# A gated mix of attention and a long convolution on one core: a planned instruction order with wider margins for loads and for TensorE's instruction blocks

## The chip, the cores and the metric

One core of a Trainium2 chip. The metric is the device time of one execution in microseconds (us); lower is better. Five engines run their own queues in order: TensorE (PE, with PEld for its weight loads), VectorE (DVE), ScalarE (ACT), GpSimd (POOL) and SyncE (SP), which here issues nearly all DMAs.

## What is computed

```python
x = A_x                                              # 1 x 2048 x 512
g = sigmoid((x * gate_w).sum(-1, keepdims=True))
# A: softmax attention, 32 heads of 16
q, k, v = split(x @ wqkv)
a = (softmax(q @ k.T / 4) @ v) @ wo
# B: a causal convolution along the sequence, one kernel of 2048 taps for each of 512 channels
K = einsum("dn,dnl,dn->dl", C, exp(dt * A * l), dt * B).real     # 128 complex poles for each channel
b = irfft(rfft(x, padded) * rfft(K, padded)) + x * Dskip         # y[t] = sum over s of K[t - s] x[s]
out = g * a + (1 - g) * b
```

## The kernel before

**Attention.** There are 32 heads x 16 key blocks of 128 x 4 query blocks of 512, that is 2,048 score tiles of 128 x 512. Three tiles make a group; there are 683 groups, numbered g. For a group, PE writes the scores into one of two banks (SC<-Qm,KT, three matmuls that run side by side), ACT takes the exponential (ET or EX<-SC, L1001), and later PE multiplies by the values into the bank OA, four matmuls of 32 columns side by side, called a quad (OA<-ET,VE). In some groups the third tile does not go to ACT: DVE makes a 16-bit exponent from the scores (DZ<-SC, L1023) and POOL makes three shifted copies (DU<-DZ, L1037). PE sums all four (OA<-DZ,VE and OA<-DU,VE). Four such tiles are a set, and it costs four quads where one would have done. So a group has an exponential of three tiles (128 x 1536) or of two (128 x 1024).

**Background.** Everything else on PE writes the one bank MB, and is put between the groups: the projections of Q, K and V, the convolution's taps (MB<-T,Z, `kstage`), the convolution itself (MB<-U,H, `ystage`; U holds 16 shifted rows of x, H the taps, and each of 32 passes v uses one U and four H, numbered u = 4v to 4v + 3) and the output (`outs`: MB<-Wo,OnR and MB<-Yl,idb, 16 row blocks lt of 128). U and H are loaded from DRAM on SP's queue (L1518, L1530) into rings; from u = 48 on the ring of H has 8 buffers, before that 4. A load is issued when the last reader of its buffer is done and, if it is paced, when a certain exponential is done. Qm is the query block with the rows of every second head zero; it is loaded from DRAM (`mk_qm`, L857), with its zeros kept in SBUF. The convolution's result goes Yst -> gm_yd -> Yl.

**What sets the order.** A planner in Python runs while the kernel is built. `Prog` keeps a clock of each engine; `Sched.fill` takes, after each group's exponential, the earliest ready piece of any thread (`ystage`, `kstage`, `outs`, ...) and appends it to its engine's queue. PE, ACT, DVE and SP run in the order so written. A load counts as landed at its reckoned end plus a margin, `DMARG` = 1.6 us. The planner also counts PE's instructions in blocks of 256; `land()` is the time at which it reckons the next block to be there. A background piece that would start with few instructions left before the block's edge is held until then:

```python
k = self.p.edge() - len(self.p.pt) - 2 * sum(isinstance(a, tuple) for a in t.seg)
if t.up > 0:
    e = max(e, self.p.land() - t.cost - max(k - KEEP, 0) / FORE)
room = max(0, want - self.p.act - own) * ZCOL
if e + t.cost + room > pe_until and t.up > 0 or e > min(until, pe_until):
    continue
```

`want` is the number of columns that PE should stream in a group (`FILL` for each 1.335 us of ACT). What lacks is filled with matmuls of zeros (OA<-wm, SC<-wm); it is set for groups below `ZEND` = 200 only. `PACE` gives by which group how many sets should have been begun; `decide` begins one when DVE's clock allows.

Of the kernel before, what the change touches and what calls it, by code (L numbers as in the profile page):

```python
# [13 lines left out]
P = 128  # L14
# [22 lines left out]
OUTP = 6  # L37
YSEG = 4
KSEG = 4
FILL = 1550  # L40
FILL2 = 1550
OVER = 0.5
# [4 lines left out]
DMARG = 1.6  # L47
SPLAG = .8
# [13 lines left out]
PACE = ((0, 0), (40, 0), (90, 0), (140, 1.0), (200, 10.0), (270, 24.0), (340, 35.9), (420, 51.9), (500, 71.9), (570, 89.4), (630, 104.4), (683, 114.47))  # L62
# [3 lines left out]
XGO = 'g30'  # L66
YGO = 'projs'
YLGO = 'K15'
BG0 = 'g0'
# [4 lines left out]
KP = 1  # L74
# [6 lines left out]
US = (2, 12, 3)  # L81
HS = (4, 48, 8)
BACK = 0.4
UN4 = 4
# [11 lines left out]
KEEP = 8  # L96
FORE = 12
# [442 lines left out]
def declare(nc, es):  # L540
# [84 lines left out]
    for n, free in (("kd", 8 * NBLK * HR * HW), ("xs", T * D * UW), ("yd", 2 * D * S), ("qd", D * S), ("od", D * S)):  # L625
        B[n] = Buf(n, "dr", free, BF16)
        B[n].t = nc.dram_tensor("gm_" + n, [free // P, P], BF16)
# [100 lines left out]
def record(nc, p, B, ins):  # L728
# [122 lines left out]
    def mk_qm(b, j):  # L851
# [575 lines left out]
    def kstage(blk):  # L1427
# [8 lines left out]
        for k in range(8):  # L1436
            for t in range(4):
# [4 lines left out]
                for j in range(4):  # L1442
                    x = k ^ j
                    ch = 32 * (blk % 4) + 4 * (j // 2) + 2 * (j % 2) + 8 * (x % 4) + x // 4
# [4 lines left out]
            if k == 0:  # L1449
                yield ("PE", .06)  # L1450
                for j in range(4):
                    mm(lambda j=j: MB(0, [[64, 4], [256, 2]], 32 * j, 32), lambda: sel(0, [[1, 32]]), lambda j=j: Dr(32 * blk + 4 * (j // 2) + 2 * (j % 2), [[8, 4], [1, 2]]),
                       [(sel, 0), (sel, 1), (Dr, 0), (Dr, 1)], ky, False, False, pos=(0, 32 * j), c=.06 if j == 0 else 0, a=2, cfg="C")
# [40 lines left out]
    UN = 4 * UW - R8 + 1  # L1494
    UP = 16 * UW // UN4

# [12 lines left out]
    def yloads():  # L1509
        yield ("AFTER", YGO)  # L1510
        for v in range(2 * NBLK):
# [4 lines left out]
            for i in range(UN4):  # L1516
                yield ("SP", .7)
                dma("SP", lambda e, v=v, U=U, i=i: e.dma_start(U(UP * i, [[1, UN]]),  # L1518
                                                               xs.dram((v // 2 * 32 + v % 2 * 4) * UW + 2 * UP * i + R8 - 1, [[D * UW, T], [-1, R8], [1, UN]])),
                    [(xs, (v // 8, s0)) for s0 in range(0, T, 4)], [(U, i, v)], c=.62, lat=3.5, b=UB * 2 / UN4, pace=True)  # L1520
            for q in range(4):
# [5 lines left out]
                for i in range(HN):  # L1527
# [3 lines left out]
                        [(kd, (u // 8, u // 2 % 4))], [(H, i, u)], c=.6, lat=3.5, b=HB / HN, pace=True)  # L1531
                sch.mark(f"yl{u}")

    def ystage():
        for u in range(2 * NBLK):
# [26 lines left out]
            op("DVE", lambda v, w=w, h=h: v.tensor_tensor(Yst(1024 * w + 4 * h, [[128, R8], [8, 16], [1, 4]]), MB(0, [[1, R8], [R8, 16], [NC, 4]]),  # L1562
# [7 lines left out]
    def yout(blk):  # L1570
# [7 lines left out]
        for k, y in enumerate((Yl, Yl2)):  # L1578
            yield ("SP", .6, YLP)
            n = 128 >> k  # L1580
            dma("SP", lambda e, k=k, y=y, n=n: e.dma_start(y(4 * n * blk, [[n, 4], [1, n]]), yd.dram(512 * blk + 8192 * k, [[8192 * 2, P], [128, 4], [1, n]])),
                [(yd, (blk, j)) for j in range(4)], [(y, blk)], c=.6, lat=3, b=.5, pace=True)
# [58 lines left out]
    def out_y(lt, bank, k, wide=False):  # L1641
        b, off, sl = bank
        y, at, W = ((Yl, 8 * lt, 128), (Yl2, 8 * (lt - 8), 64))[k]
        strips(wide, lambda p, n: b(off, [[1, 512]], p, n), lambda p, n: idb(p, [[1, n]]), lambda: y(at, [[W, D // 8], [1, 8]]),
               [(idb, 0)] + [(y, x) for x in range(NBLK)], [(b, sl, ('o', lt))], False, k == 1 and lt < 12)
# [5 lines left out]
    def outs():  # L1651
# [16 lines left out]
        for lt in range(13):  # L1668
# [13 lines left out]
            if lt < 8:  # L1682
                op("DVE", lambda v, lt=lt, o=o, off=off: v.scalar_tensor_tensor(o(off, [[1, D]]), MB(0, [[1, D]]), B["g"](lt, [[1, 1]]),
                                                                                Yl(8 * lt, [[128, D // 8], [1, 8]]), ALU.mult, ALU.add),
                   [(MB, 0, ('o', lt))] + [(Yl, k) for k in range(NBLK)] + key("g"), W, c=.7)
# [238 lines left out]
```

## Time and profile before

| | us |
|---|---|
| runs, median of 3 | 759.11 (756.84 to 760.77) |
| profiled execution | 762.17 |
| its span | 760.4 |
| ACT busy | 735.7 |
| PE busy | 688.9 |
| DVE busy | 656.1 |
| POOL busy | 363.4 |
| DMA queue q1, share of 16 engines | 49.8% |

Busy time is the sum of an engine's records. The profile calls time "issue" in which an engine waited for nothing that it shows. Rows of windows give, for each engine, its busy time and in brackets the number of its instructions, and at the end the granted TensorE clock (1.00 is full speed), the DMA share and GB/s.

### The profile page before, as it was taken

To read this page: it belongs to the slowest core of one execution; us is meant where nothing else is said; L and a number is where in the kernel's file an instruction comes from. 1 tells how busy PE (TensorE), PEld (TensorE's weight loads), DVE (VectorE), ACT (ScalarE), POOL (GpSimd) and SP (SyncE) were. 2 spreads that over 40 slices of the span, in tenths; PEclk is the share of its full clock that TensorE was granted. 3 is DMA by queue.
4 is the path that set the end of the run, shared out by engine and by line. 5 is a ranking of instruction groups with operands and counts; after the bars stand their busy time and mean duration, and the time that the engine had idled before them with its cause. 6 is when DMAs were issued, how large, how long until landed. Compare 5 with 4: busy or idle time off the path is not lost.

```text
span 760.4 us, 31203 instructions
## 1 busy us (share of the span) xinstructions
PE 688.9 (91%) x13820; PEld 288.1 (38%) x13821; DVE 656.1 (86%) x1091; ACT 735.7 (97%) x694; POOL 363.4 (48%) x358
## 2 busy tenths in 40 slices
PE   8778877987898899999999998989999999999997
PEld 3222332432454443445444433524443444222222
DVE  8999997899998898889879868988887878787884
ACT  7999999999999999999999978999999999999995
POOL 5000000100053455565536545586778777777674
PEclk9999999999999999999999989999999999999999
DMA  9656561441554767646578788216356576110001
GB/s 206 157 110 123 110 99 32 112 107 40 163 131 101 203 182 191 185 110 158 132 180 231 177 216 210 65 41 175 107 126 158 126 193 148 36 32 20 25 16 36
DMA packets 177769, 94.45 MB, mean 124 GB/s; under 512 B 117857, under 2 KB 161250, under 8 KB 177634
## 3 DMA queue, kind: packets, MB, share of 16 engines
q1 hardware_dynamic: 175618, 91.28, 49.8%
q8 instruction: 108, 1.77, 1.0%
q10 hardware_dynamic: 2016, 1.18, 0.7%
q14 instruction: 27, 0.22, 0.1%
HBM read 63.29 MB, written 18.90 MB: 108 GB/s over the span
## 4 chain that ended last, share of the span: by engine, by line
ACT 82%; PE 12%; DVE 2%; POOL 2%; DMA 1%; issue 1%; POOLq 0%; SPq 0%; DVEq 0%
ACT ET L1001 74%; ACT EX L1001 7%; PE OA L743 5%; PE SC L743 5%; PE MB L743 2%; POOL DU L1037 2%; DMA H<-gm_kd 1%; DVE DZ L1023 1%; DVE T L1082 0%; DVE ON L1073 0%; ACT L1001 0%; ACT L1773 0%; POOLq L705 0%; SPq L1530 0%; DVEq L705 0%
## 5 line engine op out<-in xcount | busy, mean ns | idle before, releaser
L1001 ACT ACTIVATE ET<-SC 128x1024 bf16<-128x1024 f32 (+1 forms) x616 | 670.9, 1369 | 10.5 <-PE SC L743 8.9
L1037 POOL INT64_ADD DU<-DZ x339 | 352.3, 1054 | 384.1 <-DVE DZ L1023 195.9
L1023 DVE TENSOR_SCALAR DZ<-SC 128x512 uint16<-128x512 f32 x452 | 302.6, 685 | 72.1 <-PE SC L743 66.1
L743 PE MATMUL SC<-Qm,KT 32*128 32x512 bf16 x2048 | 274.7, 388 | 55.7 <-ACT ET L1001 50.7
L743 PEld LDWEIGHTS SC<-Qm,KT 32*128 32x128 bf16 x2048 | 70.0, 91 | 262.3 <-ACT ET L1001 202.3
L743 PE MATMUL OA<-ET,VE 128*32 128x512 bf16 x1456 | 151.0, 392 | 0.0
L743 PE MATMUL OA<-DU,VE 128*32 128x512 bf16 x1356 | 132.0, 388 | 1.6 <-POOL DU L1037 1.5
L743 PEld LDWEIGHTS MB<-U,H 128*32 128x32 bf16 x4096 | 83.9, 144 | 29.5 <-issue 19.3
L743 PE MATMUL MB<-U,H 128*32 128x88 bf16 (+7 forms) x4096 | 91.1, 226 | 3.3 <-issue 1.7
L1001 ACT ACTIVATE EX<-SC 128x1024 bf16<-128x1024 f32 (+1 forms) x67 | 71.5, 1277 | 0.0
L1082 DVE TENSOR_TENSOR T<-B,DT 128x1536 bf16<-128x1536 bf16 x64 | 64.0, 1035 | 0.2 <-issue 0.2
L743 PEld LDWEIGHTS OA<-ET,VE 128*32 128x32 bf16 x1456 | 39.0, 95 | 59.8 <-issue 56.5
L743 PE MATMUL OA<-wm 128*32 128x256 bf16 (+3 forms) x318 | 56.0, 346 | 1.2 <-DVE idf L793 1.2
L743 PEld LDWEIGHTS OA<-DU,VE 128*32 128x32 bf16 x1356 | 35.5, 97 | 44.5 <-issue 34.2
L743 PEld LDWEIGHTS MB<-T,Z 128*32 128x32 bf16 x2048 | 44.8, 154 | 11.2 <-issue 6.9
L743 PE MATMUL MB<-T,Z 128*32 128x64 bf16 (+1 forms) x2048 | 47.5, 235 | 0.1
L743 PE MATMUL OA<-DZ,VE 128*32 128x512 bf16 x452 | 45.6, 393 | 0.0
L1082 DVE TENSOR_TENSOR ft<-Z 128x512 f32<-128x512 f32 (+3 forms) x48 | 39.4, 845 | 0.3
L1082 DVE TENSOR_TENSOR Z<-ft,ft 128x1024 bf16<-128x1024 bf16 (+3 forms) x56 | 33.1, 591 | 0.7
L1058 DVE STREAM_TRANSPOSE OT<-OA 128x512 f32<-128x512 f32 x32 | 22.7, 708 | 5.9 <-PE OA L743 5.8
L1562 DVE TENSOR_TENSOR Yst<-MB,gt 128x512 bf16<-128x512 f32 x32 | 21.8, 682 | 4.3 <-PE MB L743 4.3
L1082 DVE TENSOR_TENSOR ft<-Z,DM 128x1024 bf16<-128x1024 bf16 x32 | 22.3, 714 | 0.0
(128 smaller groups left out, 401.6 us busy)
## 6 DMA issues: line engine op xcount, KB each, us to landing
H<-gm_kd SPq DMA_DIRECT2D x128, 256.0 KB, 4.2
U<-gm_xs SPq DMA_DIRECT2D x128, 134.2 KB, 3.7
T<-B SPq DMA_DIRECT2D x16, 256.0 KB, 2.9
gm_yd<-Yst SPq DMA_DIRECT2D x64, 64.0 KB, 2.8
gm_kd<-Ks SPq DMA_DIRECT2D x64, 40.0 KB, 2.8
gm_xs<-xP SPq DMA_DIRECT2D x16, 136.0 KB, 4.3
gm_pd<-L SPq DMA_DIRECT2D x8, 256.0 KB, 4.3
Z<-gm_pd SPq DMA_DIRECT2D x8, 256.0 KB, 3.6
```

What stands on the lines that cost most here:

```text
L743: op("PE", lambda t: t.matmul(out(), lhsT(), rhs(), start=start, stop=stop, skip_group_check=True, **kw), R, W, c=c, lat=.15, a=a, cfg=cfg)
L1001: op("ACT", lambda a: a.activation(E(at, [[1, 512 * n]]), sc(0, [[1, 512 * n]]), AF.Exp, scale=DH ** -0.5), [(sc, i, g) for i in range(n)] ...
L1023: op("DVE", lambda v: v.tensor_scalar(z.u16(512 * k, [[1, 512]]), sc(1024, [[1, 512]]), XS, XB, ALU.mult, ALU.add), [(sc, 2, g)], [(z, k, ...
L1037: op("POOL", lambda v, u=u, cut=cut: v.int64_add(u.u64(), z.u64(), cut * 0x0001000100010001), R, [(u, 0, i)], c=1.016, lat=.09, lk=True)
L1058: op("DVE", lambda v: v.transpose(OT(512 * w, [[1, 512]]), OA(0, [[1, 512]])), [(OA, 0, b)], [(OT, w, b)], c=.64)
L1082: op(eng, lambda v: v.tensor_tensor(o(), a(), b_(), f), R, W, c=c)
L1562: op("DVE", lambda v, w=w, h=h: v.tensor_tensor(Yst(1024 * w + 4 * h, [[128, R8], [8, 16], [1, 4]]), MB(0, [[1, R8], [R8, 16], [NC, 4]]), ...
```

## The change

The change alters the planner's numbers, some transfers and the layout of three buffers; the whole order is then planned anew.

- Numbers: `KEEP` 8 to 36 and `FORE` 12 to 15, so that a background piece is held back when fewer than 36 instructions of the block would be left, not 8. `FILL` 1550 to 1500, `OVER` 0.5 to 0.3. From group 200 on `want` is no longer 0 but follows `LOW` = 1150, with a surplus of up to `SURP` = 1200 columns carried over. `PACE` is changed; 114 sets are begun, not 113. Priorities (`OUTP`, `KP`) and starts (`XGO`, `BG0`, `YLGO`) are changed.
- The margin of U loads from v = 12 and of H loads from u = 48 on is `HM` = 5 us.
- Qm comes by one transfer of 128 rows, not four of 16; its zero rows lie in DRAM, written by four new transfers (`qzeros`). U comes in two pieces of 1081 columns, not four of 537. Yl is loaded in two halves with shorter runs, 64 transfers and not 32. The channels are put in another order for this (`ch`, Yst, Yl).

```diff
-FILL = 1550
-FILL2 = 1550
-OVER = 0.5
+FILL = 1500
+FILL2 = 1500
+OVER = 0.3
+LOW = 1150
+SURP = 1200
+HM = 5
-UN4 = 4
+UN4 = 2
-KEEP = 8
-FORE = 12
+KEEP = 36
+FORE = 15
...
     def mk_qm(b):
-            dma("SP", lambda e: e.dma_start(Qm(512 * w, [[1, 512]], 32 * j + 16 * w, 16),
-                                            B["qd"].dram(((4 * qc + pi) * P + 32 * j + 16 * w) * 512, [[512, 16], [1, 512]])),
-                [(B["qd"], (pi, qc))], [(Qm, (w, j), b)], c=.62, lat=2.8)
+            dma("SP", lambda e: e.dma_start(Qm(512 * w, [[1, 512]]),
+                                            B["qd"].dram((2 * (4 * qc + pi) * P + 16 * w) * 512, [[64 * 512, 4], [512, 32], [1, 512]])),
+                [(B["qd"], (pi, qc)), (B["qd"], ('z', qc))], [(Qm, (w, j), b) for j in range(4)], c=.55, lat=2.9, b=.45)
...
     def yloads():
-                                                               xs.dram((v // 2 * 32 + v % 2 * 4) * UW + 2 * UP * i + R8 - 1, [[D * UW, T], [-1, R8], [1, UN]])),
-                    [(xs, (v // 8, s0)) for s0 in range(0, T, 4)], [(U, i, v)], c=.62, lat=3.5, b=UB * 2 / UN4, pace=True)
+                                                               xs.dram(16 * v * UW + UP * i + R8 - 1, [[D * UW, T], [-1, R8], [1, UN]])),
+                    [(xs, (v // 8, s0)) for s0 in range(0, T, 4)], [(U, i, v)], c=.62, lat=3.5, b=UB * 2 / UN4, m=HM if v >= US[1] else DMARG, pace=True)
-                        [(kd, (u // 8, u // 2 % 4))], [(H, i, u)], c=.6, lat=3.5, b=HB / HN, pace=True)
+                        [(kd, (u // 8, u // 2 % 4))], [(H, i, u)], c=.6, lat=3.5, b=HB / HN, m=HM if u >= HS[1] else DMARG, pace=True)
...
     def yout(blk):
-            n = 128 >> k
-            dma("SP", lambda e, k=k, y=y, n=n: e.dma_start(y(4 * n * blk, [[n, 4], [1, n]]), yd.dram(512 * blk + 8192 * k, [[8192 * 2, P], [128, 4], [1, n]])),
+            n = 64 >> k
+            for h in range(2):
+                dma("SP", lambda e, k=k, y=y, n=n, h=h: e.dma_start(y(4 * n * (2 * blk + h), [[n, 4], [1, n]]), yd.dram(512 * blk + 8192 * k + 64 * h, [[8192 * 2, P], [128, 4], [1, n]])),
...
+    def qzeros():
+        for c in range(4):
+            yield ("AFTER", QZ[c])
+            yield ("SP", .6, 1)
+            dma("SP", lambda e, c=c: e.dma_start(B["qd"].dram((8 * c * P + 16) * 512, [[32 * 512, 32], [512, 16], [1, 512]]), wm(0, [[0, 16], [1, 512]], 0, 32)),
+                [(wm, 0)], [(B["qd"], ('z', c))], c=.6, lat=3.5, b=2.0, pace=c > 0)
...
     for g in range(NG):
-        want = (FILL if g < REST[3] else FILL2) * (t - t0) / 1.335 + min(max(lack, -256), 768)
+        want = (FILL if g < ZEND else LOW) * (t - t0) / 1.335 + min(max(lack, -256 if g < ZEND else -SURP), 768)
-        sch.fill(t, t + OVER, want if g < ZEND else 0)
-        lack = want - p.act if g < ZEND else 0
+        sch.fill(t, t + OVER, want)
+        lack = want - p.act
```

The order of the queues changes all over the program. Three places follow; buffer numbers stand behind the names.

The first is SP's queue where loads 76 to 79 of H are issued (H4 to H7), with U1 of their pass ahead of them. Before:

```order
L1518 DMA U1_161<-gm_xs 128x1x537 x2
L1574 DMA gm_yd<-Yst_171 32x8x128 x4
L1518 DMA U1_161<-gm_xs 128x1x537 x2
L1530 DMA H4_167<-gm_kd 128x1x1024
L1530 DMA H5_168<-gm_kd 128x1x1024
L1530 DMA H6_169<-gm_kd 128x1x1024
L1530 DMA H7_170<-gm_kd 128x1x1024
L1518 DMA U2_162<-gm_xs 128x1x537 x2
L857 DMA Qm_52<-gm_qd 16x512 x4
L1518 DMA U2_162<-gm_xs 128x1x537 x2
```

and after:

```order
L1522 DMA U1_161<-gm_xs 128x1x1081
L1751 DMA gm_qd<-wm_89 32x16x512
L1522 DMA U1_161<-gm_xs 128x1x1081
L1534 DMA H4_167<-gm_kd 128x1x1024
L861 DMA Qm_52<-gm_qd 128x1x512
L1534 DMA H5_168<-gm_kd 128x1x1024
L1534 DMA H6_169<-gm_kd 128x1x1024
L1534 DMA H7_170<-gm_kd 128x1x1024
L1578 DMA gm_yd<-Yst_171 32x8x128 x4
L1522 DMA U2_162<-gm_xs 128x1x1081 x2
```

The issues of U and Qm have become fewer rows of the same bytes or more, and a new write of zeros (gm_qd<-wm) stands among them. By the planner's group numbers H4 is issued in group 359 and first read in 364 before; it is issued in 362 and first read in 380 after.

The second is PE's queue at the convolution's loads 84 and 85 (H4 and H5, with U0). Before (groups 382 and 383):

```order
L743 MATMUL MB<-U0_160,H4_167 32x72 x4
L743 MATMUL SC0<-Qm_52,KT_49 128x512 x3
L743 MATMUL MB<-U0_160,H5_168 32x128 x4
L743 MATMUL MB<-U0_160,H5_168 32x120 x4
L743 MATMUL MB<-U0_160,H5_168 32x112 x4
L743 MATMUL MB<-U0_160,H5_168 32x104 x4
L743 MATMUL MB<-U0_160,H5_168 32x96 x4
L743 MATMUL MB<-U0_160,H5_168 32x88 x4
L743 MATMUL MB<-U0_160,H5_168 32x80 x4
L743 MATMUL MB<-U0_160,H5_168 32x72 x4
L743 MATMUL MB<-U0_160,H6_169 32x128 x4
L743 MATMUL MB<-U0_160,H6_169 32x120 x4
```

and after (groups 397 to 400):

```order
L747 MATMUL OA<-DU02_60,VE_53 32x512 x4
L747 MATMUL SC1<-Qm_52,KT_49 128x512 x3
L747 MATMUL MB<-U0_160,H4_167 32x96 x4
L747 MATMUL MB<-U0_160,H4_167 32x88 x4
L747 MATMUL MB<-U0_160,H4_167 32x80 x4
L747 MATMUL MB<-U0_160,H4_167 32x72 x4
L747 MATMUL OA<-DU03_61,VE_53 32x512 x4
L747 MATMUL SC0<-Qm_52,KT_49 128x512 x3
L747 MATMUL OA<-ET_54,VE_53 32x512 x4
L747 MATMUL OA<-DU00_58,VE_53 32x512 x4
L747 MATMUL SC1<-Qm_52,KT_49 128x512 x3
L747 MATMUL OA<-DZ01_57,VE_53 32x512 x4
```

Before, 64 convolution matmuls stand in a row behind the scores SC0, of which the first 40 and more are shown; after, runs of 16 stand with two or three score groups between them.

The third is the end of PE's queue, from the last score group on. Before:

```order
L743 MATMUL SC0<-Qm_52,KT_49 128x512 x2
L743 MATMUL OA<-DZ13_65,VE_53 32x512 x4
L743 MATMUL MB<-Wo_79,OnT3_72 32x512 x8
L743 MATMUL OA<-DU13_69,VE_53 32x512 x4
L743 MATMUL MB<-Yl_101,idb_93 32x512 x4
L743 MATMUL OA<-ET_54,VE_53 32x512
L743 MATMUL OA<-EX_55,VE_53 32x512 x3
L743 MATMUL MB<-Yl2_102,idb_93 32x512 x4
L743 MATMUL OA<-DU14_70,VE_53 32x512 x4
L743 MATMUL OA<-DU15_71,VE_53 32x512 x4
L743 MATMUL SC1<-Wo_79,OnT3_72 128x512 x3
L743 MATMUL OA<-EX_55,VE_53 32x512 x4
```

and after:

```order
L747 MATMUL OA<-DU13_69,VE_53 32x512 x4
L747 MATMUL MB<-Wo_79,OnR2_75 32x512 x4
L747 MATMUL MB<-Yl_101,idb_93 32x512 x4
L747 MATMUL MB<-Yl2_102,idb_93 32x512 x4
L747 MATMUL OA<-DU14_70,VE_53 32x512 x4
L747 MATMUL OA<-ET_54,VE_53 32x512 x4
L747 MATMUL OA<-DU15_71,VE_53 32x512 x4
L747 MATMUL MB<-Wo_79,OnT3_72 32x512 x12
L747 MATMUL MB<-Yl_101,idb_93 32x512 x4
L747 MATMUL MB<-Yl2_102,idb_93 32x512 x4
L747 MATMUL SC1<-Wo_79,OnT3_72 128x512 x3
L747 MATMUL OA<-ET_54,VE_53 32x512 x4
```

The output's matmuls into MB for row block 12 (OnT3, Yl, Yl2) stood ahead of the last two sums (DU14, DU15); they now stand behind them, since row block 11 is only finished there.

More of the change, by code (lines that the diff above doesn't have):

```diff
@@ L65 @@
 YQ = 0
-XGO = 'g30'
+XGO = 'g50'
 YGO = 'projs'
-YLGO = 'K15'
-BG0 = 'g0'
+YLGO = 'K14'
+BG0 = 'g30'
 BG1 = 'K1'
@@ L73 @@
 TP = 2
-KP = 1
+KP = 0.2
 NB = 2
@@ L80 @@
 NZ = 2
-US = (2, 12, 3)
-HS = (4, 48, 8)
+US = [2, 12, 3]
+HS = [4, 48, 8]
 BACK = 0.4
-UN4 = 4
+UN4 = 2
+QZ = ('g6', 'g80', 'g200', 'g360')
 HN = 1
@@ L1561, in ystage @@
             yield ("DVE", .7, -1)
-            op("DVE", lambda v, w=w, h=h: v.tensor_tensor(Yst(1024 * w + 4 * h, [[128, R8], [8, 16], [1, 4]]), MB(0, [[1, R8], [R8, 16], [NC, 4]]),
+            op("DVE", lambda v, w=w, h=h: v.tensor_tensor(Yst(1024 * w + 64 * h, [[128, R8], [4, 16], [1, 4]]), MB(0, [[1, R8], [R8, 16], [NC, 4]]),
                                                 B["gt"](0, [[16, R8], [1, 16], [0, 4]]), ALU.mult),
@@ L1642, in out_y @@
         b, off, sl = bank
-        y, at, W = ((Yl, 8 * lt, 128), (Yl2, 8 * (lt - 8), 64))[k]
-        strips(wide, lambda p, n: b(off, [[1, 512]], p, n), lambda p, n: idb(p, [[1, n]]), lambda: y(at, [[W, D // 8], [1, 8]]),
-               [(idb, 0)] + [(y, x) for x in range(NBLK)], [(b, sl, ('o', lt))], False, k == 1 and lt < 12)
+        y, at, W = ((Yl, 4 * lt, 64), (Yl2, 4 * (lt - 8), 32))[k]
+        strips(wide, lambda p, n: b(off, [[1, 512]], p, n), lambda p, n: idb(p, [[1, n]]), lambda: y(at, [[W, D // 4], [1, 4]]),
+               [(idb, 0)] + [(y, (x, h)) for x in range(NBLK) for h in range(2)], [(b, sl, ('o', lt))], False, k == 1 and lt < 12)
     def out_dma(lt, q="SP"):
```

35 lines of the change are left out of this document (18 added, 17 removed).

## The prediction

> **What bounds the kernel now.** I read the page first (busy shares, chain), then the exponentials by shape, then ACT's and PE's time line where ACT stands idle, then the clock window by window. "L1001" is the exponential of the scores, SC the score banks, OA the attention sums, MB the bank of all other matmuls, which I call background.
>
> ```profile
> PE 688.9 (91%) x13820; PEld 288.1 (38%) x13821; DVE 656.1 (86%) x1091; ACT 735.7 (97%) x694; POOL 363.4 (48%) x358
> ACT 82%; PE 12%; DVE 2%; POOL 2%; DMA 1%; issue 1%; POOLq 0%; SPq 0%; DVEq 0%
> ```
>
> ACT bounds: 97% busy and 82% of the chain. The groups of ACT by shape, then pieces of the chain and of ACT's time line (start, length, count):
>
> ```profile
> L1001 ACT ACTIVATE ET<-SC 128x1024 bf16<-128x1024 f32 x392 | 378.4, 1190 | 9.4 <-PE SC L743 7.9 <-PE OA L743 1.1
> L1001 ACT ACTIVATE ET<-SC 128x1536 bf16<-128x1536 f32 x224 | 310.2, 1682 | 1.1 <-PE SC L743 1.0
> L1001 ACT ACTIVATE EX<-SC 128x1024 bf16<-128x1024 f32 x61 | 63.3, 1239 | 0.0
> L1001 ACT ACTIVATE EX<-SC 128x1536 bf16<-128x1536 f32 x6 | 9.6, 1672 | 0.0
> ...
> 11.18 1.45 ACT ET L1001
> 13.15 57.76 ACT ET L1001 x43
> 569.13 6.42 ACT ET L1001 x7
> 746.42 3.54 ACT L1001 ACTIVATE EX<-SC 128x1024 bf16<-128x1024 f32 x3
> ```
>
> Records overlap, so the pace is read from unbroken runs: 57.76/43 = 1.343 us for three tiles, 6.42/7 = 0.917 us for two. 453 exponentials of two and 230 of three need 415.4 + 308.9 = 724.3 us. They run from 11.18 to 746.42 + 3.54 = 749.96, 738.8 us, of which some 0.8 is two small ACT instructions. So 13.7 us are lost between them; 11.2 before and 10.4 behind are head and tail of the 760.4 us span.
>
> Where the 13.7 us lie: ACT in two stretches of 100 us, and the shapes in the second.
>
> ```profile
> 280.00:380.00 100.00, 99.53 (x99) 1.00 0.60 153
> 380.00:480.00 100.00, 91.89 (x90) 0.93 0.79 199
> L1001 ACT ACTIVATE ET<-SC 128x1024 bf16<-128x1024 f32 x68 | 65.6, 1086 | 7.5 <-PE SC L743 6.7 <-PE OA L743 0.7
> L1001 ACT ACTIVATE ET<-SC 128x1536 bf16<-128x1536 f32 x22 | 31.4, 1525 | 0.6 <-PE SC L743 0.5
> ```
>
> 68 x 0.917 + 22 x 1.343 = 91.9: 8.1 us are lost from 380 to 480, where the granted clock is 0.93. The other 640 us lose 5.6, some 0.9 in 100. What stopped PE there, from the time lines of SP, PE and ACT (last bracket: idle before, and releaser) and the chain:
>
> ```profile
> 387.19 4.67 DMA H<-gm_kd
> 433.53 3.10 SPq L1530 DMA_DIRECT2D H<-gm_kd  x4
> 437.73 0.45 PE L743 MATMUL MB<-U,H 128*32 128x128 bf16 x16 [1.72 <-issue]
> 438.54 1.97 ACT L1001 ACTIVATE ET<-SC 128x1024 bf16<-128x1024 f32 x2 [1.47 <-PE SC L743]
> 460.11 1.14 PE L743 MATMUL MB<-U,H 128*32 128x128 bf16 x64
> 464.87 0.39 PE L743 MATMUL SC<-Qm,KT 32*128 32x512 bf16 x2 [0.69 <-issue]
> ```
>
> The reader is to see two causes. First, a convolution matmul stands in PE's queue ahead of scores and waits for its H: issued at 433.53, used at 437.73, 4.2 us later; the chain has the same wait from 387.19. Second, behind a burst of 64 background matmuls PE stands 0.69 us for "issue" in the middle of three scores, which wait for no data that the profile shows. The clock then adds to both (PE busy is the first figure, granted clock the third from the end):
>
> ```profile
> 67.95:71.36 3.41, 2.20 (x30) 0.65 (x26) 3.37 (x6) 3.41 (x4) 0.00 (x0) 1.00 0.60 85
> 71.36:74.78 3.42, 3.42 (x35) 0.85 (x32) 2.48 (x5) 3.42 (x3) 0.00 (x0) 0.50 0.17 21
> 95.26:98.67 3.41, 2.25 (x70) 1.01 (x57) 3.36 (x7) 3.41 (x4) 0.00 (x0) 1.00 0.13 12
> ...
> 388.80:392.22 3.42, 2.04 (x35) 0.67 (x34) 3.35 (x7) 3.42 (x4) 0.00 (x0) 1.00 0.79 189
> ...
> 436.59:440.00 3.41, 2.07 (x70) 1.42 (x70) 1.65 (x3) 1.94 (x3) 3.03 (x3) 1.00 1.07 252
> 463.90:467.31 3.41, 2.03 (x14) 0.48 (x12) 2.77 (x6) 2.69 (x3) 2.80 (x3) 1.00 0.42 121
> 467.31:470.72 3.41, 3.41 (x27) 0.76 (x30) 2.07 (x5) 2.21 (x3) 1.30 (x2) 0.50 0.91 235
> ```
>
> A stretch of 3.41 us with PE busy for 2.0 to 2.2 is followed by one at half clock; the row of 2.25 is the lowest that is not. From 380 to 480 a clock of 0.93 is 7 us of full clock missing, four such stretches of 1.7, after the three rows that stand there.
>
> **The change, part by part.** (1) One more set of tiles goes from ACT to DVE (114 sets for 113). The program has 457 exponentials of two tiles and 226 of three: 419.1 + 303.5 = 722.6, so -1.7 us on the path. What the set adds elsewhere, by the page:
>
> ```profile
> L1037 POOL INT64_ADD DU<-DZ x339 | 352.3, 1054 | 384.1 <-DVE DZ L1023 195.9 <-DVE T L1082 95.9 <-DVE ft L1082 41.1
> L1023 DVE TENSOR_SCALAR DZ<-SC 128x512 uint16<-128x512 f32 x452 | 302.6, 685 | 72.1 <-PE SC L743 66.1
> H<-gm_kd SPq DMA_DIRECT2D x128, 256.0 KB, 4.2
> U<-gm_xs SPq DMA_DIRECT2D x128, 134.2 KB, 3.7
> Yl<-gm_yd SPq DMA_DIRECT2D x16, 128.0 KB, 3.1
> Yl<-gm_yd SPq DMA_DIRECT2D x16, 64.0 KB, 3.3
> DMA to landing us min/median/max: 3.1/4.2/6.8
> ```
>
> DVE gets 4 x 0.685 = 2.7 us, POOL 3 x 1.054 = 3.2, PE three quads of matmuls. DVE is 86% and POOL 48% busy, so ACT covers them; without that cover they would be the 2.7 us.
>
> (2) Loads are asked for earlier (HM). The last row is H alone, issue to landing. Counted in score groups between an H load's place in SP's order and its first matmul, 14 of the 80 loads from number 48 on have 5 or 6 groups before, 4.6 to 5.5 us at 0.917; now three have 7 (6.4 us), 77 have 8 or more. So nearly all stand beyond the 6.8 us maximum. SP is relieved: 120 + 128 + 32 = 280 issues of Qm, U and Yl become 30 + 64 + 64, with four of zeros, all in the queue that issues H. A U of double size should land near H's 4.2 us (256 KB); its nearest first use is 6 groups off. The 32 more Yl loads land in 3.1 to 3.3 us by the two rows of half and full size, and are first read 5.9 us of exponentials later: nothing on the path. Qm now comes in one transfer, 17 us of exponentials ahead of its use.
>
> (3) Background is held back near the end of a block of PE's instructions (KEEP, FORE), and LOW keeps it spread. Groups with 48 or more convolution matmuls fall from 16 to 10. Counted over 3.41 us of exponentials, the lowest share of the array's columns in use rises from 0.32 to 0.37. No zero matmul stands past group 199 in either program, so the "floor" works by spacing alone.
>
> (2) and (3) act on the same 8.1 us; lower bound of their gain 0, upper 8.1. I take 7.2: the stretch then loses 0.9 like the rest, because each of its three places starts with a wait that the counts above remove.
>
> (4) The tail gets worse. The order of PE now puts five quads (three of OnT, two of Yl) behind the last DU quad, where before they stood ahead of it:
>
> ```profile
> 748.64 0.39 PE L743 MATMUL OA<-DU,VE 128*32 128x512 bf16 x4
> 748.86 0.42 PE L743 MATMUL MB<-Yl,idb 128*32 128x512 bf16 x4
> ...
> 750.41 0.40 PE L743 MATMUL OA<-DU,VE 128*32 128x512 bf16 x4 [0.48 <-POOL DU L1037]
> 751.95 0.72 DVE L1058 STREAM_TRANSPOSE OT<-OA 128x512 f32<-128x512 f32 x1 [4.96 <-PE OA L743]
> ```
>
> A quad takes 748.86 - 748.64 = 0.22 us. DVE's last transpose waits for PE, so +5 x 0.22 = +1.1. Bounds: 0 if POOL's last sum comes later than PE's other work allows, 1.8 if the cast of 0.7 us that now frees MB first is late as well.
>
> Head, Yst's new strides (same size) and the earlier K stage: nothing, they lie beside exponentials. If they are late, (2)'s rest of 0.9 grows.
>
> Sum against the profiled execution, 762.17 us: -1.7 - 7.2 + 1.1 = 754.4. Its median of runs is 759.11, 3.1 lower, so part of the losses that I take away was perhaps not in the other runs; the remaining losses should vary less. I take a third of that difference: 753.5.
>
> **Rivals.** A, slower. FILL goes from 1550 to 1500 and zero columns before group 200 from 32,640 to 27,904. One window at half clock costs ACT
>
> ```profile
> 66.26 8.67 ACT L1001 ACTIVATE ET<-SC 128x1536 bf16<-128x1536 f32 x6
> 75.43 1.45 ACT L1001 ACTIVATE ET<-SC 128x1536 bf16<-128x1536 f32 x1 [0.50 <-PE SC L743]
> ```
>
> 75.43 - 66.26 - 6 x 1.343 = 1.1 us. There are 54 windows before 195 us, one fell. 4,736 columns at 512 in 0.22 us are 2.0 us, 0.04 a window, and only the window of 2.25 is that near to 2.20; I expect none or one more. It decides from nine new ones on (753.5 + 9.9 = 763.4). Against it: the lows are few. The Trainium skill (TensorE: Matmul & The Clock Gate, Part 1, "What's actually happening") gives half clock after at least one idle window of about 3.4 us; by that rule PE, never idle so long here, would not slow and rival A could not happen, the sum staying 753.5. The trace disagrees: PE was busy 2.20 of 3.41 us and still fell to 0.50. So A keeps a chance, 0.07.
>
> B, no change: the waits move. H loads below number 48 still have 5 or 6 groups in 13 cases, 64 matmuls in a row still stand in three groups, and the POOL sums that PE waits for are as dense. If all 8.1 us come back elsewhere: 762.17 - 1.7 + 1.1 = 761.6, less the 3.1 of the median 758.5. Chance 0.22.
>
> C, half: H is cured, the instruction wait is not. The place from 463.90 keeps its ACT idle, 3.41 - 2.69 and 3.41 - 2.21, 1.9 us, plus what the overlap of records hides, 0.3: 755.7. Chance 0.15.
>
> **How the numbers follow.** Forecast 0.56, C 0.15, B 0.22, A 0.07. A measurement here tells 0.5%, 3.8 us: faster is below 755.3, slower above 762.9. Faster: 0.47 of the forecast's 0.56, since its own spread passes 755.3, 0.06 of C, 0.05 of B: 0.58. Slower: A and 0.02 of B's spread, 0.09. Same: 0.33. Range: low end all 8.1 and half of the other 5.6 regained with the whole 3.1 of the median, 762.17 - 1.7 - 8.1 - 2.8 + 1.1 - 3.1 = 747.6; high end B and 1 us for its spread, 759.5.
>
> **What would show it.** Right: ACT's 100 us from 380 on hold 99 us or more of work, no PE wait on H above 0.5 us past load 48, at most two windows at 0.50, the last transposition starting 2.5 us or more behind the last DU quad (1.54 before). Wrong: half-clock windows before 195 us (A); new idle of ACT for PE with H or POOL as PE's releaser (B); "issue" between the scores of one group again (C); or a Yl or U load that a matmul waits for.

## The result: 0.76% slower, not 0.7% faster

| | before | changed |
|---|---|---|
| median of 14 runs each, us | 759.18 (756.84 to 763.21) | 764.48 (760.53 to 771.0) |
| profiled execution, us | 762.17 | 764.41 |
| its span | 760.4 | 762.6 |

The ratio of the changed kernel to the one before is 1.0076, 95% interval 1.0049 to 1.0104. It was repeated later (e15): 1.0089 (1.0058 to 1.0119). The changed kernel's profile lies at its median. That of before was, as the prediction said, 3 us above its own.

The page of the changed kernel, first the busy times, then the chain, then the two groups of the convolution's taps (weight load and matmul); below them the same two groups of before:

```profile
PE 693.7 (91%) x13770; PEld 297.5 (39%) x13770; DVE 658.7 (86%) x1095; ACT 736.3 (97%) x694; POOL 366.8 (48%) x361
ACT 67%; PE 25%; DVE 4%; DMA 1%; issue 1%; POOL 1%; ACTq 0%; DVEq 0%; SPq 0%; POOLq 0%
L747 PEld LDWEIGHTS MB<-T,Z 128*32 128x32 bf16 x2048 | 52.2, 178 | 10.0 <-issue 6.6
L747 PE MATMUL MB<-T,Z 128*32 128x64 bf16 (+1 forms) x2048 | 53.2, 243 | 0.0
```

```profile
L743 PEld LDWEIGHTS MB<-T,Z 128*32 128x32 bf16 x2048 | 44.8, 154 | 11.2 <-issue 6.9
L743 PE MATMUL MB<-T,Z 128*32 128x64 bf16 (+1 forms) x2048 | 47.5, 235 | 0.1
```

ACT still bounds, but PE's share of the chain went from 12% to 25%: PE is late more often. It has 50 instructions fewer and is busy 4.8 us longer. Of PE's large groups of instructions only those of the taps became slower by the piece: 178 ns for a weight load instead of 154, with the same shapes and the same number.

By the prediction's own terms the span of 762.6 us is made of 11.6 us of head (11.2 before), 722.6 of exponentials at their pace (724.3), 16.1 lost between them (13.7), 0.8 for two small ACT instructions and 11.4 of tail (10.4). So the floor fell by 1.7 as forecast, the tail rose by 1.0 (forecast 1.1), and the losses, which were to fall by 7.2, rose by 2.4.

ACT's busy time in three stretches of 100 us (then count, granted clock, DMA share, GB/s). Changed:

```profile
280.00:380.00 100.00, 97.63 (x95) 0.98 0.60 155
380.00:480.00 100.00, 95.61 (x93) 0.97 0.76 203
480.00:580.00 100.00, 97.01 (x102) 0.98 0.44 103
```

Before, the third stretch (the other two stand in the prediction: 99.53 and 91.89):

```profile
480.00:580.00 100.00, 98.67 (x105) 1.00 0.44 111
```

The stretch that the change aimed at gained 3.7 us of ACT against this profile of before, the one ahead of it lost 1.9 and the one behind it 1.7. One profile each carries little: in the second profiles (e1 of before, e15 of the changed kernel) the three stretches hold 98.55, 93.28 and 97.81 us, and 98.91, 94.81 and 97.02. How a loss looks now, on the time line of the changed kernel:

```profile
391.77 0.32 PE L747 MATMUL MB<-U,H 128*32 128x80 bf16 x8 [0.49 <-issue]
392.24 0.69 DVE L1566 TENSOR_TENSOR Yst<-MB,gt 128x512 bf16<-128x512 f32 x1 [0.61 <-PE MB L747]
395.76 0.39 PE L747 MATMUL SC<-Qm,KT 32*128 32x512 bf16 x1 [0.60 <-DVE DZ L1027]
397.85 0.22 PE L747 MATMUL MB<-U,H 128*32 128x72 bf16 x1 [0.43 <-issue]
398.65 1.02 ACT L1005 ACTIVATE ET<-SC 128x1024 bf16<-128x1024 f32 x1 [0.76 <-PE SC L747]
```

No wait for H is left. At 391.77 PE waits for its own instructions ("issue"; a packet of the instruction queue q8 had started 2.6 us before), so DVE, whose queue is in order, waits for MB at 392.24. Its conversions DZ come late, and at 395.76 a score has to wait until DZ frees the score bank. At 397.85 PE waits for instructions once more, and a window at half clock follows. Over the whole kernel, the scores' waits for DZ (us, times, longest), before and changed:

```profile
PEld SC L743 <- DVE DZ L1023: 4.2, 12, 1.0
PE SC L743 <- DVE DZ L1023: 0.5, 2, 0.2
```

```profile
PEld SC L747 <- DVE DZ L1027: 10.8, 26, 1.3
PE SC L747 <- DVE DZ L1027: 3.0, 7, 0.8
```

That is 4.7 us before and 13.8 now. So there were four suspects: the dearer taps, DVE being late, the planner's new numbers, and a gain that was never there.

### The profile page after: what moved, and what is told of

Read it like the earlier page. It is cut to its first block, busy times and chain, and to the rows that moved or that the text cites. A ratio compares the mean times of both kernels' runs of the same rounds, so it can differ in the third digit from the quotient of the medians.

```text
span 762.6 us, 30962 instructions
## 1 busy us (share of the span) xinstructions
PE 693.7 (91%) x13770; PEld 297.5 (39%) x13770; DVE 658.7 (86%) x1095; ACT 736.3 (97%) x694; POOL 366.8 (48%) x361
## 4 chain that ended last, share of the span: by engine, by line
ACT 67%; PE 25%; DVE 4%; DMA 1%; issue 1%; POOL 1%; ACTq 0%; DVEq 0%; SPq 0%; POOLq 0%
ACT ET L1005 62%; PE SC L747 10%; PE OA L747 10%; PE MB L747 5%; ACT EX L1005 5%; DVE DZ L1027 2%; DMA Wk<-in_A_wqkv_dram 1%; POOL DU L1041 1%; DVE T L1086 0%; DVE Yst L1566 0%; DMA Yl<-gm_yd 0%; DVE Kt L1460 0%; DVE OT L1062 0%; ACTq L751 0%; DVE Z L1086 0%
## 5 line engine op out<-in xcount | busy, mean ns | idle before, releaser
L747 PEld LDWEIGHTS MB<-U,H 128*32 128x32 bf16 x4096 | 86.6, 143 | 30.0 <-issue 18.7
L747 PE MATMUL MB<-U,H 128*32 128x128 bf16 (+7 forms) x4096 | 94.1, 225 | 2.5 <-issue 2.5
L1005 ACT ACTIVATE EX<-SC 128x1024 bf16<-128x1024 f32 (+1 forms) x65 | 67.8, 1214 | 0.3
L747 PEld LDWEIGHTS MB<-T,Z 128*32 128x32 bf16 x2048 | 52.2, 178 | 10.0 <-issue 6.6
L747 PE MATMUL MB<-T,Z 128*32 128x64 bf16 (+1 forms) x2048 | 53.2, 243 | 0.0
L747 PE MATMUL OA<-wm 128*32 128x256 bf16 (+3 forms) x267 | 51.1, 350 | 1.2 <-DVE idf L797 1.2
L1484 POOL MEMSET xP<- 128x256 bf16 x4 | 1.7, 460 | 62.6 <-DVE DM L1141 62.6
```

Of the source, the lines that this page charges most:

```text
L747: op("PE", lambda t: t.matmul(out(), lhsT(), rhs(), start=start, stop=stop, skip_group_check=True, **kw), R, W, c=c, lat=.15, a=a, cfg=cfg)
L1005: op("ACT", lambda a: a.activation(E(at, [[1, 512 * n]]), sc(0, [[1, 512 * n]]), AF.Exp, scale=DH ** -0.5), [(sc, i, g) for i in range(n)] ...
L1484: op("POOL", lambda v, k=k: v.memset(xP(k * T * XW, [[XW, T], [1, 16]]), 0.0), [], [(xP, (0, k))], c=.45)
```

## The experiments

Ratios are to the kernel before, run on the same chip, with 95% intervals. Runs without a ratio are single runs. A changed constant makes the planner write a new order for all engines. Edits inside an instruction (a width, an address) keep the order, and these are the ones that isolate a cause.

**e1, before again**, no edit.

> The kernel before once more, unchanged. Its first profile was 762.17 us, 3.0 above the median of its 14 runs (759.18). Theory H (the waits for H loads at 387 and 437 us, with the half clock behind them, are in every run of before, so the change did take 7 to 8 us away and something else took more): the second profile shows both waits again, PE waiting more than 0.5 us for each, and a loss of ACT of 6 us or more between 380 and 480 us. Rival S (they were one run's bad luck, and the prediction counted a gain that the median run had no room for): the second profile lies near 759, at least one of the two waits is under 0.3 us, and the loss from 380 to 480 us is 5 us or less. Times: ratio 1.000, within 0.3%, either way.

Measured: 0.9989 (0.996 to 1.0019); its profiled run took 764.04 us. Both waits are there, at the same two places:

```profile
392.74 0.75 PE L743 MATMUL MB<-U,H 128*32 128x128 bf16 x32 [0.86 <-DMA H<-gm_kd]
438.71 0.44 PE L743 MATMUL MB<-U,H 128*32 128x128 bf16 x16 [1.95 <-issue]
```

ACT is busy for 93.28 of the 100 us from 380 on, so it loses 6.7. Theory H holds for the waits: they were no accident of one run. For their size it is not shown. This profile's run is 5.3 us above its median of 758.69, as that of before was 3.0 above. Three kernels that keep before's order and whose DZ is whole (e6, e7, e12) hold 96.99, 96.10 and 95.70 us of ACT in that stretch, so they lose 3.0 to 4.3 there, and e7, whose run took 759.32 us, still has the second wait, 1.72 us at 435.68. So part of the prediction's 8.1 us belongs to a run that lay above the median.

**e2 and e3, short DZ** in the changed kernel and in the kernel before; the orders stay:

```diff
+        wd = 512 if all(x["z"] is not z for x in sets[:i]) else 256
-        op("DVE", lambda v: v.tensor_scalar(z.u16(512 * k, [[1, 512]]), sc(1024, [[1, 512]]), ...
+        op("DVE", lambda v: v.tensor_scalar(z.u16(512 * k, [[1, wd]]), sc(1024, [[1, wd]]), ...
```

> The changed kernel in the same order, but DVE converts only half of each DZ tile after a buffer's first use (256 columns, some 0.37 us instead of 0.68; the sums then use stale halves). Theory D (DVE is now the one that is late: scores wait for DZ to free a score bank, 13.8 us in 33 waits against 4.7 in 14 before, and the quiet windows behind them get the half clock): the waits of scores for DZ fall under 2 us, the time falls by 4 us or more, to about 760 or below, and further than the same edit takes the kernel before. Rival F (the waits start with PE waiting for its own instructions, at 391.8, 397.9, 461.4 and 467.2 us, 2.5 us in all, and DVE is only where they show): the four waits of 'issue' stay, half-clock windows stay, and the time falls by less than 2 us.

> The same halved DZ in the kernel before: the control for the halved DZ in the changed kernel. Theory D: before had 4.7 us of such waits and POOL behind DVE, so it gains 0.5 to 2 us (757 to 759). If it gains as much as the changed kernel (4 us or more), then short DZ helps both alike and is not what tells them apart.

Measured: changed 758.76 us, 1.0002 (0.9975 to 1.0029); before 755.89 us, 0.9948 (0.9927 to 0.9969). The edit takes 0.74% from the changed kernel and 0.52% from the one before. The waits for DZ fall to 2.3 us in the changed kernel. (The sums then use stale halves of DZ.) Theory D gets some 0.2% of the difference, about 1.7 us, which the intervals don't tell from nothing. The rest, 0.54% between the two with short DZ, is not DVE's lateness.

**e4, transfers and layouts alone**: the changed code with every number of the planner as before (PACE, KEEP, FORE, FILL, OVER, OUTP, starts, HM = 1.6; from group 200 on no columns are asked for).

> The changed kernel's transfers and layouts (Qm in one DMA with its zeros in DRAM, U in two pieces, Yl in two halves) with all numbers of the planner as before (PACE, KEEP, FORE, FILL, OVER, OUTP, starts, margin 1.6). Theory N (the planner's new numbers, above all PACE and the holding back, make it slower; the transfers cost nothing): 757 to 760 us, ratio 0.998 to 1.001. Rival T (the transfers and layouts cost: T,Z matmuls take 243 ns instead of 235, their weight loads 178 instead of 154, the head 0.45 us more): ratio 1.004 or more, with T,Z loads near 178 ns.

Measured: 774.54 us, 1.0189 (1.0159 to 1.022). Theory N falls. Both signs of rival T are there, the ratio and weight loads of 179 ns for the taps, but the order is another one as well:

```profile
PEld SC L747 <- DVE DZ L1027: 15.3, 35, 1.5
PEld OA L747 <- POOL DU L1041: 13.9, 30, 3.2
```

The last exponential ends 13.8 us ahead of the end. So it is a bad plan besides, and the price of the transfers can't be read from it. What it gave was the hint: the slow taps came with the layout, not with the numbers.

**e5, e6 and e7, the taps' addresses.** Four matmuls of a step, j = 0 to 3, run side by side in the four column groups; each reads its own column `ch` of Z (weights) and of T (moving). The edits change which x goes with which j, so the same products are formed in another sequence, and the planner's order stays. In e5 (changed kernel) and e6 (before):

```diff
-                    x = k ^ j
+                    x = k ^ (0, 2, 1, 3)[j]     # e5
+                    x = k ^ (0, 4, 1, 5)[j]     # e6
```

> The changed kernel with one number per matmul of the taps changed: the four column groups j of a step take x = k ^ (0, 2, 1, 3)[j] and not k ^ j. The order of every engine stays, the result too. The change's new channel order lets two of the four reads that run side by side fall into one 32-byte piece of T (ch 0 and 6 at k = 0: bytes 0 and 24); with this edit all four lie in different pieces, as in the kernel before (ch 0, 10, 20, 30: bytes 0, 40, 80, 120). Theory R (T,Z matmuls follow each other in 17.1 ns instead of 13.9, by the records' starts in runs of nine and more, because of the pairs; 2,048 of them are 6.6 us of PE, and this is most of what the change lost): the spacing returns to 14 ns, the weight loads of T,Z from a mean of 178 to 154 ns, and the time falls by 3 us or more, to 761.5 or below. Rival P (the spacing has another cause, such as neighbours in the new order, or PE has room for it): spacing stays near 17 ns, or the time stays within 1.5 us of 764.5.

> The reverse in the kernel before: x = k ^ (0, 4, 1, 5)[j], so that two of the four side-by-side reads fall into one 32-byte piece (ch 0 and 1 at k = 0). Order and result stay. Theory R: spacing of T,Z goes from 13.9 to 17 ns and the time rises by 2 to 5 us, to 761 to 764. Rival P: spacing and time stay (759 to 760).

> Which operand it is: the kernel before, where only the moving operand T is read at the paired offsets; the weights Z keep theirs (so taps are wrong). Theory R names the moving reads: spacing of T,Z near 17 ns. If it is the weight loads (Z pairs lie 12 bytes apart after, 20 before): spacing stays at 13.9 ns.

Measured: e5 760.23 us, 1.0028 (1.0006 to 1.005); e6 765.42 us, 1.0081 (1.0059 to 1.0104); e7, where only T is read at the paired offsets, 759.32 us in one run. The spacing of T,Z matmuls (mean distance of their starts in unbroken runs) is 13.9 ns in e5, 17.1 in e6 and 14.1 in e7. Theory R holds for the effect and falls for its place: it is not the moving reads alone.

**e12 and e14, the weight reads alone**, in the kernel before: T as it was, and Z read at the paired offsets (e12) or with the same x for all four j (e14); the taps then mix channels.

```diff
+                    y = k ^ (0, 4, 1, 5)[j]     # e12; (0, 0, 0, 0) in e14
+                    wc = 32 * (blk % 4) + 4 * (j // 2) + 2 * (j % 2) + 8 * (y % 4) + y // 4
-                    ... lambda ch=ch, t=t: Z(t // 2 * 4096 + ch, [[128, 32]]),
+                    ... lambda wc=wc, t=t: Z(t // 2 * 4096 + wc, [[128, 32]]),
```

> The kernel before with only the weight reads of the taps (Z) at the paired offsets, the moving reads as they were (so taps are wrong). With the moving reads alone paired the spacing was 14.1 ns (13.9 before, 17.1 with both paired). If the weight loads are the cause: spacing near 17 ns and weight loads of T,Z near a mean of 179 ns. If it takes both together: near 14 ns again.

> How far the price of the weight reads goes: in the kernel before all four weight reads of a step fall into one 16-byte piece (the same x for all j; taps are wrong). Two in one piece gave 16.9 ns between T,Z matmuls, none 13.9. If reads of one piece go one after the other: 22 to 28 ns, 17 to 28 us more of PE, and 770 us or more. If one shared piece is as dear as two: 17 to 18 ns, near 761.

Measured: e12 761.01 us with a spacing of 16.9 ns and weight loads of 180 ns; e14 808.18 us with some 26 ns and 241 ns. It is the weight loads that became dearer. (The time of e12 says little: before took 757.20 to 762.27 us on that chip.) The time lines show the price directly: 64 weight loads T,Z, and the first load of the scores behind them. In turn before, changed, e5, e7, e12 and e14:

```profile
150.89 1.11 PEld L743 LDWEIGHTS MB<-T,Z 128*32 128x32 bf16 x64 [0.23 <-issue]
152.04 0.09 PEld L743 LDWEIGHTS SC<-Qm,KT 32*128 32x128 bf16 x1
```

```profile
321.67 1.34 PEld L747 LDWEIGHTS MB<-T,Z 128*32 128x32 bf16 x64 [0.23 <-issue]
323.04 0.10 PEld L747 LDWEIGHTS SC<-Qm,KT 32*128 32x128 bf16 x3
```

```profile
321.18 1.08 PEld L747 LDWEIGHTS MB<-T,Z 128*32 128x32 bf16 x64 [0.23 <-issue]
322.31 0.10 PEld L747 LDWEIGHTS SC<-Qm,KT 32*128 32x128 bf16 x3
```

```profile
150.44 1.15 PEld L743 LDWEIGHTS MB<-T,Z 128*32 128x32 bf16 x64 [0.23 <-issue]
151.62 0.09 PEld L743 LDWEIGHTS SC<-Qm,KT 32*128 32x128 bf16 x1
```

```profile
151.55 1.40 PEld L743 LDWEIGHTS MB<-T,Z 128*32 128x32 bf16 x64 [0.23 <-issue]
152.99 0.09 PEld L743 LDWEIGHTS SC<-Qm,KT 32*128 32x128 bf16 x1
```

```profile
210.04 2.04 PEld L743 LDWEIGHTS MB<-T,Z 128*32 128x32 bf16 x64 [0.23 <-issue]
212.68 0.10 PEld L743 LDWEIGHTS SC<-Qm,KT 32*128 32x128 bf16 x3 [0.61 <-ACT ET L1001]
```

From the first row to the second, divided by 64: 18.0 ns before, 21.4 changed, 17.7 with spread reads, 18.4 with only the moving reads paired, 22.5 with only the weights paired. In e14 the scores behind waited for an exponential, so there it is the loads' own 2.04 us, 32 ns. For 2,048 matmuls, 3.4 ns are 7 us of PE; of that, spread reads (e5) gave back 0.48% of the time, 3.6 us.

That PE is late is only part of how it costs time. In e14 14 ns are 29 us of PE, but the time rose by 49 us, and ACT stood idle for the scores less than before. ACT's exponentials into ET were busy 48.9 us longer, though they are the same in number and size. Below are this group in before and e14, and, from the chains of before, e6 and e14, the same 121 exponentials, which follow each other without a wait:

```profile
L1001 ACT ACTIVATE ET<-SC 128x1024 bf16<-128x1024 f32 (+1 forms) x616 | 670.9, 1369 | 10.5 <-PE SC L743 8.9
85.03 151.93 ACT ET L1001 x121
```

```profile
85.75 154.66 ACT ET L1001 x121
```

```profile
L1001 ACT ACTIVATE ET<-SC 128x1024 bf16<-128x1024 f32 (+1 forms) x616 | 719.8, 1468 | 6.4 <-PE SC L743 5.2
84.09 176.59 ACT ET L1001 x121
```

The exponentials themselves are slower, and only those that run beside weight loads of the taps. From end to end, in unbroken runs, one of three tiles takes 1.34 us in all these kernels with none of these loads beside it. With them it takes 1.35 before and in e5, 1.36 in the changed kernel, 1.40 in e12, 1.46 in e6 and 2.17 in e14; one of two tiles 0.92, 0.92, 0.93, 0.92, 0.95 and 1.42. Added up in the unbroken runs, that is 47 of e14's 49 us, some 5.5 of e6's 6.2 and 1.2 in the changed kernel. So in before's order nearly all of the price is paid by ACT directly. In the changed kernel that is a third of the 3.6 us, and the rest shows as late scores: 33 exponentials start over 0.06 us after the one before them ended, 10.7 us in all, and 24 with 7.9 us in e5. What ACT and the weight loads share, no run shows; nor why e6, with T paired as well, costs ACT more than e12.

The addresses: Z's elements have 2 bytes, so `ch` = 0, 10, 20, 30 (before, k = 0) lie at bytes 0, 20, 40, 60, each in a 16-byte piece of its own. The new order has 0, 6, 24, 30, at bytes 0 and 12, 48 and 60: two pieces for four readers. In e6 they are two, at bytes 0, 6, 24 and 30 (`ch` 0, 3, 12 and 15; the expectation's 0 and 1 is a slip). With e5's x the pieces are four again. Pairs share a 32-byte piece in before and e5 too, at no price, so 32 is too wide; and 8 is too narrow, since the four reads of the changed kernel lie in four pieces of 8. That two readers of one 16-byte piece wait for each other fits all these kernels; what is inside the reading port no run shows.

**e8, outputs last** (spread reads; `OUTP` 1 to 6).

> The changed kernel with the spread reads and, besides, OUTP back from 1 to 6 (outputs are put last again; this replans the order). After's tail, from the end of the last exponential to the end, is 11.4 us against 10.4 before, because quads of output stand ahead of the last sums. Theory T (that is OUTP's doing): tail 10.4 to 10.6, time 0.5 to 1.5 us below the kernel with the spread reads alone. Rival: outputs crowd the last groups under OUTP 6 as well, tail 11 or more and no gain.

Measured: 761.4 us, 1.0042 (1.0024 to 1.0059). The tail is 13.0 us. Theory T falls, the rival holds: this priority alone does not shorten the tail, in an order planned anew.

**e9, the load margin alone**, in the kernel before:

```diff
+HM = 5
-  ... b=UB * 2 / UN4, pace=True)
+  ... b=UB * 2 / UN4, m=HM if v >= US[1] else DMARG, pace=True)
-  ... b=HB / HN, pace=True)
+  ... b=HB / HN, m=HM if u >= HS[1] else DMARG, pace=True)
```

> The kernel before with one part of the change alone: U loads from v = 12 and H loads from u = 48 on count as landed 5 us after their reckoned end, not 1.6 (replanned; 453 exponentials of two tiles and 230 of three as before). In the order, the H loads from 48 on with 5 or 6 groups to their first matmul go from 14 of 80 to none (one with 7). Theory M (the wait for H was real, but its price in the median run is small, and what PE then waits for comes next): PE's waits for H go, 1.9 us; time 756.5 to 759, at most 0.3% below before. The prediction's step (2)+(3): the wait and the half clock behind it are the 8.1 us of that stretch: 751 to 754. Rival W (asked for earlier, conv matmuls stand later and crowd): 760 or more.

Measured: 759.03 us, 1.0005 (0.9983 to 1.0026). No wait for H is left, and nothing is gained, which the interval (1.6 us either way) tells from the 7.2 us of the prediction. That is theory M. Its profile is of a run 5.0 us above the median, so it shows what can come next and not what a median run loses. What PE waits for there stands in the middle of a run of 16 matmuls of one H, where no data can be missing; in the trace a packet of the instruction queue (q8) starts at 413.78, 2.2 us earlier:

```profile
414.13 0.29 PE L744 MATMUL MB<-U,H 128*32 128x128 bf16 x6
415.99 0.38 PE L744 MATMUL MB<-U,H 128*32 128x120 bf16 x10 [1.57 <-issue]
416.73 1.02 ACT L1002 ACTIVATE ET<-SC 128x1024 bf16<-128x1024 f32 x1 [1.08 <-PE SC L744]
```

ACT's busy time is 94.79 from 380 to 480 (91.89 before) but 96.49 from 480 to 580 (98.67), and the tail is 11.8 us (10.4).

**e10 and e11, the changed kernel with spread reads**, once with KEEP = 8 and FORE = 12, once with HM = 1.6.

> The changed kernel with the spread reads of the taps and KEEP and FORE back to 8 and 12 (replanned). Theory K (holding background back until the instruction block is reckoned landed does not remove the instruction waits, four of 0.4 to 0.8 us in the changed kernel, and makes DVE and the sums late): time 1.5 us or more below the changed kernel with the spread reads (ratio to before 1.001 or less), fewer groups in which PE is overfull. The prediction's step (3): without the holding back the instruction waits come back, two or more of 0.7 us with half clock behind, 1 to 3 us slower (ratio 1.004 to 1.007).

> The changed kernel with the spread reads and the margin HM back from 5 to 1.6 (the order is the same up to group 319). H loads from 48 on keep 7 groups or more with either margin, since SP's queue now has fewer issues. Theory M: within 1.5 us of the changed kernel with the spread reads (ratio 1.001 to 1.005). The prediction's step (2): waits for H at 390 to 440 us return and it is 2 us or more slower.

Measured: e10 774.03 us, 1.0188 (1.0159 to 1.0217). The last exponential ends at 750.0 of 772.4, a tail of 22 us: the output's matmuls were pushed behind the exponentials.

```profile
ACT fo L1900 <- PE SC L747: 17.6, 1, 17.6
```

Theory K isn't borne out: without the holding back the kernel is slower, and the last exponential ends 4.1 us later than in e5 (745.9), tail aside. The prediction's step (3) isn't shown either: most of the time went into a tail, and the order is another one from early on. e11: 761.88 us, 1.0034 (1.0008 to 1.0059), the same as e5 within the intervals. The margin of 5 us is worth nothing measurable here.

**e13 and e15**: both order-keeping edits, spread reads and short DZ, in the changed kernel; and the changed kernel again, on one chip.

> The changed kernel in its own order with both edits: spread reads of the taps and DZ half as long (the sums use stale halves). With short DZ alone it was 0.02% above before, with spread reads alone 0.28% above; the kernel before with short DZ was 0.52% below. Theory D2 (the 0.28% that the spread reads leave is DVE's lateness): at least as fast as the kernel before with short DZ, ratio 0.993 to 0.995 (753.5 to 755.5). Rival O (it is PE's overfull groups and the tail, which DVE has no part in): 0.2 to 0.4% above that kernel, ratio 0.997 to 0.999, tail still 11.4 us.

> The changed kernel once more, unchanged, beside the two others on one chip. Ratio to before 1.005 to 1.010 as in the first comparison (1.0076); the two T,Z numbers again 178 ns for a weight load and 17 ns of spacing; tail 11.4 us; scores waiting for DZ 10 us or more in all.

Measured: e13 757.77 us, 0.9977 (0.9954 to 1.0001); e15 766.07 us, 1.0089 (1.0058 to 1.0119), with weight loads of 178 ns, a spacing of 17.1 ns and 13.8 us of waits for DZ. e13 lies 0.29% above before with short DZ, as much as e5 lies above before. Rival O's numbers hold: what the spread reads leave over is not DVE's lateness. That it is overfull groups of PE isn't shown.

No kernel tried here that computes the whole result beats the one before.

## Why the prediction was wrong, point by point

- **A step that failed: the channel order was put at nothing.** The prediction set the layouts at nothing ("Yst's new strides (same size)": "nothing") and priced of the new order of channels only what it does to DVE and DMA. It did not look at what `ch` does to the four weight reads that run side by side. e5 against the changed kernel gives 1.0076 - 1.0028 = 0.48% (some 0.35 either way, by the two intervals), 3.6 us; against e15 it is 0.61%. e6 makes a loss of the same kind, 0.81%, in the kernel before. It is paid twice: PE is late, and exponentials beside the loads are slower. DVE's lateness may be in part a consequence: short DZ saves 0.74% with the pairs (e2) and 0.51% with spread reads (e13 against e5), where before it saves 0.52%; the intervals don't separate these. The Trainium skill (TensorE: Matmul & The Clock Gate, Part 2, "Step-by-step: what each phase is for") has the time of a weight load scale with its column count. Here 32 columns took 154, 178 or 241 ns, by the addresses alone, so the measurement decides.
- **(2) and (3), 7.2 us: gone, not gained.** This is the other step that failed, and the largest term of the sum. The waits were real (e1) and the margin removes them (e9: no wait for H is left), but the time stays at 1.0005. Two things were wrong. The 8.1 us were read from a run 3.0 us above the median; kernels in before's order lose 3.0 to 4.3 there in other runs (e6, e7, e12). And the stretch was to lose 0.9 "like the rest" once the waits are gone, but in the changed kernel it loses 4.4 (5.2 in e15): this is the mechanism of rival B, "the waits move". There is an instruction wait of 1.57 us in e9, and there are four of 0.4 to 0.8 us in the changed kernel at 391.8, 397.9, 461.4 and 467.2 us. The granted clock did not rise: on one chip (e15) it is 0.993 in the mean of 17 runs of before and 0.991 in the 6 of the changed kernel.
- **Rival C** was right in its mechanism. 'issue' inside a burst is what is left when H is cured, and KEEP = 36 does not prevent it. `LOW` and `SURP` do nothing at all: without them the planner writes the same program, so the prediction's "LOW keeps it spread" is wrong.
- **(1), -1.7 us:** right; 457 and 226 exponentials, and nothing late by the set itself that the runs can separate.
- **(4), +1.1 us:** right. 1.0 us more of tail, by the mechanism named, on the changed kernel's time line:

```profile
751.53 0.40 PE L747 MATMUL OA<-DU,VE 128*32 128x512 bf16 x4
751.99 0.83 PE L747 MATMUL MB<-Wo,OnT 128*32 128x512 bf16 x12
752.65 0.75 PE L747 MATMUL MB<-Yl,idb 128*32 128x512 bf16 x8
754.08 0.40 PE L747 MATMUL OA<-ET,VE 128*32 128x512 bf16 x4
754.54 0.72 DVE L1062 STREAM_TRANSPOSE OT<-OA 128x512 f32<-128x512 f32 x1 [2.60 <-PE OA L747]
```

  The last transposition starts 3.0 us behind the last DU quad (forecast 2.5 or more, 1.54 before), since the five quads stand between. The cast that frees MB, which the prediction had as its upper bound, was late too: the first load of Wo waits 0.37 us for it.
- **"What would show it":** no wait for H past load 48, right. ACT's 99 us from 380 on, wrong: 95.61. At most two windows at half clock, wrong: there are four, one at 329.5, two from 397.7, one at 554.8. None came before 195 us, so rival A did not happen.
- **The sum** by what is measured, in per cent of 759: pairs of weight reads 0.48, the rest 0.28 (0.06 to 0.50), which is 2.1 us. In that rest are -1.7 of floor, +1.0 of tail and some +0.3 of head (the first exponential starts at 11.5 us on average in eight profiles of before's order, at 11.8 in eight of the changed kernel and its variants, e4 left out). So about 2.5 us of losses between exponentials remain unexplained (0.9 to 4.2 by that interval). They are not DZ (e13) and not the margin (e11). The profiles don't show them: exponentials that start over 0.06 us after the one before them number 24, 27 and 26 in e5, e8 and e11, and 22 and 27 in the two profiles of before. The prediction's other parts in the new order were not tried by themselves, and this stays open.

## What to carry to other kernels

When a change moves data in SBUF, price the instructions that read it, not only those that move it: compare the mean time of one instruction by group before and after, since a group with the same shapes and a longer mean is the change's own doing. Look at the other engines' groups beside it too: here reads of PE made ACT's exponentials slower. Size a gain from a run at the median, not from one 3 us above it. A wait seen in the profile is worth what the run gains without it, not its length plus all that follows; in a program whose order is planned as a whole, the next wait stands close behind. To find a cause there, use edits that keep the order (an address, a width), because a changed constant moves everything and cost up to 15 us here for reasons of its own.

## What the runs showed of the hardware that was not expected

- Weight loads of matmuls in the four column groups slow each other when they read the same 16-byte piece of each partition row: 18 ns a matmul with four pieces, 21 to 23 with two, 32 with one (128 rows, 32 columns, a step of 256 bytes). The moving reads at paired offsets cost next to nothing by themselves (18.4).
- Such loads slow another engine. ACT's exponentials of three tiles took 1.35 us beside loads from four pieces, 1.36 to 1.46 with two, and 2.17 with one, against 1.34 with none beside them (one or two profiles of each kernel).
- The prediction read from before that a window of 3.41 us with PE busy for 2.0 to 2.2 is followed by half clock. In the changed kernel the windows ahead of the three drops were (PE busy first, granted clock third from the end):

```profile
326.06:329.47 3.41, 2.95 (x37) 0.89 (x31) 3.41 (x7) 2.87 (x4) 2.23 (x3) 1.00 0.24 82
394.33:397.74 3.41, 2.50 (x85) 1.53 (x82) 3.26 (x6) 3.06 (x4) 0.75 (x1) 1.00 0.93 263
551.34:554.75 3.41, 2.60 (x29) 0.69 (x25) 3.41 (x7) 3.08 (x4) 1.98 (x2) 1.00 0.00 0
```

  So busy time alone does not tell which window is followed by a drop: 2.95 of 3.41 was. The idle window that the Trainium skill asks for (TensorE: Matmul & The Clock Gate, Part 1, "What's actually happening") is not there either. What does, these runs do not settle.
- An instruction wait of PE ended 2.2 to 3.3 us after the start of a packet of the instruction queue (five places in the changed kernel and e9). The first two of these places in the changed kernel are 126 matmuls apart and the last two 127, where a block of 256 instructions holds at most 128 pairs of load and matmul; e5 and e13 have waits at the same matmuls as the last three.
